# A recurrence that feeds a soft mixture of experts on one core: the last gate moved, one more buffer, the drain put in another order

## The chip, the cores and the metric

The kernel runs on one core of a Trainium2 chip. The core has five engines that run side by side and meet at semaphores: TensorE (PE; its weight loads are listed as PEld), VectorE (DVE), ScalarE (ACT), GpSimd (POOL) and SyncE (SP). SP issues the plain transfers, POOL those that convert float32 to bfloat16 on the way. The metric is the device time of one execution in microseconds (us), as the median of several; lower is better. All other times are us counted from the start of the span of one profiled execution.

## The reference

```python
def _attn_ref(x, f_logit, lower_bound):
    B, S, D = x.shape                                # 4, 5056, 256
    sig = 1.0 / (1.0 + np.exp(-f_logit))
    f = lower_bound + (1.0 - lower_bound) * sig
    i = 1.0 - f
    for t in range(S):
        h = f[:, t] * h + i[:, t] * x[:, t]
        y[:, t] = h
    return y

def _moe_ref(x, phi, w1, w2):                        # x: (20224, 256), E = 8, F = 1024
    logits = x @ phi                                 # 32 slots, 4 for each expert
    d = softmax(logits, axis=0)                      # over all tokens
    slot_input = (d.T @ x).reshape(E, S_per_e, D)
    for e in range(E):
        h = np.maximum(slot_input[e] @ w1[e], 0.0)
        slot_out[e] = h @ w2[e]
    c = softmax(logits, axis=1)                      # over the slots
    return c @ slot_out.reshape(n_slots, D)
```

The softmaxes are written out in the reference; they are shortened here. The output of the recurrence, for all four batches, is the input of the mixture. Because the first softmax runs over all tokens, no output token can be written before the last token has gone through the recurrence and all experts have been computed.

## The kernel before

**Tiling.** The 5056 steps of a batch are cut into 10 groups of 512 (128 partitions times R = 4 steps), the ninth (`odd`, group 8) holding 448. A unit is one group of one batch; unit n is group n // 4 of batch n % 4, 40 units in all. Units are loaded in pairs.

**The steps of a unit**, each a small function: `load` (SP: f_t and x_t, three buffers each), `gate` (ACT: sigmoid of f_t for a pair into s_t), `enter` (POOL: u_t = s_t * x_t), `s_to_channels` and `u_to_channels` (PE: transposes into sp, one buffer of two units, and up, two buffers), `decay` (ACT: a = 1 - (1 - lower_bound) * s, for a pair, one instruction for each half of the channels), `scan` (DVE: the recurrence itself, two instructions, into a buffer of `hpool`), `to_tokens` (PE: transposes of h back, into hp, which has one buffer) and `keep_tokens` (a copy of hp into ht, on DVE for even batches and on ACT for odd ones).

**The steps of a group**: `logits` (PE: phi against h), `exps` (ACT: exponentials for two groups in one instruction, with a table load before them and another when the sigmoid comes back), `weights_to_tokens` (PE transposes, DVE copy into et) and `slots` (PE: accumulates slot_ps).

**The order is written out by hand.** The body of the loop over n names what is issued at step n; each engine executes its own instructions strictly in the order of that text, so a waiting instruction holds up all behind it on its engine. `W_AT` says at which step POOL issues how many of the 16 expert weights (8 of w1, called w0 to w7 below, and 8 of w2, called w8 to w15), each 1 MB of float32 that becomes 0.5 MB of bfloat16. At step 34 the gate of units 38 and 39 and the exponentials of groups 6 and 7 stand ahead of `decay` of 36 and 37, which follows at step 35. `spin` issues matmuls whose results nobody reads.

**The drain** begins with the last scan: logits, exponentials and weights of the last group in two parts (three batches, then the fourth), `left_over` (the 64 odd steps of group 8, four small ACT copies), the last slots, `row_sums` (PE: the denominators of the second softmax), the slot inputs (slot_sb, sin), the w1 products and relu, transposes into `hid`, and the w2 products. Experts 0 to 5 are computed on 32 rows, four at a time, into so4_ps, and are repeated to 128 rows by a matmul with rep; the last W = 2 experts go straight to 128 rows through `wide`, a zeroed array into which their columns are copied. slot_out is the result, on 128 partitions.

**The output**: for each unit, four matmuls of slot_out with the kept exponentials, a scaling on DVE or ACT, and a store by SP.

The lines named below: L183 gate, L194 enter, L209 transposes to channels, L232 decay, L242 scan, L253 and L262 to_tokens and keep_tokens, L286 exps, L121 and L123 weight loads, L128 spin, L554 and L568 w2 products, L572 slot_out, L595 to L632 output.

Of the kernel before, what the change touches and what calls it, by code (L numbers as in the profile page):

```python
# [18 lines left out]
def kernel(  # L19
# [93 lines left out]
    slot_sb = store.tile([P, D], F32, name="slot_sb")  # L113
# [17 lines left out]
    W_AT = {12: 1, 18: 1, 24: 1, 29: 1, 32: 1, 34: 3, 35: 1, 36: 7}  # L131
# [6 lines left out]
    with tc.tile_pool(name="ld", bufs=3) as ld, \  # L138
         tc.tile_pool(name="sp2", bufs=3) as sp2, \
         tc.tile_pool(name="sup", bufs=4) as sup, \  # L140
         tc.tile_pool(name="apool", bufs=2) as apool, \
         tc.tile_pool(name="hpool", bufs=7) as hpool, \
# [6 lines left out]
        slot_ps = pslot.tile([P, D], F32, name="slot_ps")  # L149
# [97 lines left out]
        def to_tokens(n):  # L247
            g, b = divmod(n, B)
            n_p = rows(g)
            hp = ptp.tile([P, R, P], F32, name="hp", tag="tp")  # L250
            hw = hs[n].bitcast(F32).rearrange("c (p r) o -> c p (r o)", r=R)
            for r in range(R):
                nc.tensor.transpose(hp[:n_p, r], hw[:, :n_p, r], ident_f)  # L253
            if b == 0:
                hts[g] = htok.tile([P, B, R, D], BF16, name="ht", tag="ht")
            hps[n] = hp
# [12 lines left out]
        def logits(g, bs=range(B)):  # L269
            T = rows(g) * R  # L270
            gs = batch_of(g)
            if g == gs[0] and bs[0] == 0:
                lgs[0] = plg.tile([P, 2 * G], F32, name="lg", tag="lg")
            lg = lgs[0][:, ds((g - gs[0]) * G, T)]
            for o in range(DC):
                for b in bs:
                    nc.tensor.matmul(lg[ds(b * NS, NS), :], phi[:, o],  # L277
                                     hs[g * B + b][:, :T, o],
                                     start=o == 0, stop=o == DC - 1,
                                     skip_group_check=True)  # L280
# [36 lines left out]
        def left_over():  # L317
            for b in range(B):
                k = ds(b * NS, NS)
                nc.scalar.copy(left[k, :, b % 2], etall[k, ds(odd * G + P * R3, L)])  # L320
# [29 lines left out]
        def late_exps(bs):  # L350
            k = ds(bs[0] * NS, len(bs) * NS)
            nc.scalar.activation(etall[k, ds(last * G, G)], lgs[0][k, :G], ACT.Exp,
                                 accum_out=csum[k, ds(last, 1)])

        def late_weights(bs, copy):
            k, w = ds(bs[0] * NS, len(bs) * NS), len(bs) * NS
            ew = etall[k, ds(last * G, G)].rearrange("s (p r) -> s p r", r=R)
            if bs[0] == 0:
                ets[last] = etok.tile([P, R, B, NS], BF16, name="et", tag="et")
            for r in range(R):  # L360
                nc.tensor.transpose(late_ps[:, r, k], ew[:, :, r], ident[k, k])
            copy(ets[last][:, :, ds(bs[0], len(bs))].rearrange("p r b s -> p r (b s)"),
                 late_ps[:, :, k])

# [26 lines left out]
        for n in range(n_unit):  # L391
# [13 lines left out]
            else:  # L405
                if n % 2 == 0:
                    unit(load, n + AHEAD)
                    unit(gate, n + 4)
                else:
                    unit(decay, n + 1)  # L410
                if n == 34:
                    exps(7)
                elif n != 33:
                    group(exps, n - 2)
# [5 lines left out]

                unit(to_tokens, n - 1)
# [3 lines left out]
                unit(u_to_channels, n + 1)  # L425
                group(logits, n - 1)
            if n == n_unit - 1:
                tail = psp.tile([P, 2, G], F32, name="tail", tag="sp")
                rs_ps = tail[:, 0, ds(0, n_grp * R * B)].rearrange(
                    "p (g r b) -> p g r b", r=R, b=B)  # L430
                late_ps = tail[:, 1].bitcast(BF16)[:, ds(0, R * P)].rearrange(
                    "p (r s) -> p r s", r=R)
                logits(last, [0, 1, 2])
                late_exps([0, 1, 2])
                for g in range(4):
                    row_sums(g)
                late_weights([0, 1, 2], nc.scalar.copy)
                spin(lgs[0][:, ds(G, G)], 2)

            if n in (n_unit - 3, n_unit - 2):  # L440
                spin(lgs[0][:, ds(G, G)], 3)
# [4 lines left out]
            if n == 35:  # L446
                weights_to_tokens(7)
            elif n != 34:
                group(weights_to_tokens, n - 3)
            if n == 36:  # L450
                slots(6)
            elif n == 37:
                slots(7)
            elif n != 35 and n != n_unit - 1:
                batch(slots, n - 4, 0)
                batch(slots, n - 4, 1)
        logits(last, [3])
        late_exps([3])
        left_over()
        to_tokens(n_unit - 1)  # L460
        nc.vector.tensor_copy(hts[last][:, B - 1].rearrange("p r d -> p (r d)").bitcast(F32),
                              hps.pop(n_unit - 1).rearrange("p r c -> p (r c)"))
        late_slots([0, 1])
        late_weights([3], nc.vector.tensor_copy)
        slots(last - 1)
        late_slots([2])
        late_slots([3])
        for g in range(4, n_grp):
            row_sums(g)
        nc.vector.tensor_copy(slot_sb, slot_ps)  # L470

    slot_out = store.tile([P, D], BF16, name="slot_out")
    with tc.tile_pool(name="ew", bufs=1) as ew, \
# [3 lines left out]
        hid = ew.tile([P, FC, E, NS], BF16, name="hid")  # L477
        nc.gpsimd.memset(hid.rearrange("p f e s -> p (f e s)"), 0.0)
        W = 2
        wide = ew.tile([P, FC, W, B, NS], BF16, name="wide")  # L480
        nc.gpsimd.memset(wide.rearrange("p f w b s -> p (f w b s)"), 0.0)
        rep2 = rep.rearrange("p b s -> p (b s)")

        sin_ps = pm.tile([P, DC, NS], F32, name="sin_ps", tag="pm")
        slot_v = slot_sb.rearrange("p (c o) -> p o c", o=DC)
        for o in range(DC):
            nc.tensor.matmul(sin_ps[:, o], slot_v[:, o], rep2[:, :NS],
                             start=True, stop=True, skip_group_check=True)
        spin(tail[:, 1], 3)
        sin = ew.tile([P, DC, NS], BF16, name="sin")  # L490
        for o in range(DC):
            nc.vector.tensor_scalar_mul(sin[:, o], sin_ps[:, o], omlb[:, ds(o, 1)])

        cs1 = ew.tile([P, 1], F32, name="cs1")
        nc.vector.tensor_reduce(cs1, csum, AX.X, ALU.add)

# [21 lines left out]
        nc.tensor.matmul(cs_ps, rep2, cs1, start=True, stop=True)  # L518
        spin(tail[:, 1], 2)
        for q in range(E // Q):  # L520
            ht_ps = psu.tile([P, FC, P], BF16, name="ht_ps", tag="up")
            hi_v = his[q].rearrange("p (c f) -> p f c", f=FC)
            for fc in range(FC):
                nc.tensor.transpose(ht_ps[:, fc], hi_v[:, fc], ident)
            spin(tail[:, 1], 2)

            src = ht_ps.rearrange("p f (j s) -> p f j s", s=NS)[:, :, :, ds(0, SPE)]
            src = bass.AP(tensor=src.tensor, offset=src.offset + q * Q * SPE,
                          ap=[list(src.ap[0]), [P, FC], [NS + SPE, Q], [1, SPE]])
            dst = hid[:, :, ds(q * Q, Q), ds(0, SPE)]  # L530
            dst = bass.AP(tensor=dst.tensor, offset=dst.offset + q * Q * SPE,
                          ap=[list(dst.ap[0]), [E * NS, FC], [NS + SPE, Q], [1, SPE]])
            if q == 0:
                nc.scalar.copy(dst, src)
            else:
                nc.vector.tensor_copy(dst, src)
            for w in range(W):
                e = E - W + w
                if e // Q == q:
                    src = ht_ps[:, :, ds((e % Q) * NS + e * SPE, SPE)]  # L540
                    nc.scalar.copy(wide[:, :, w, :, ds(e * SPE, SPE)],
                                   src.unsqueeze(2).broadcast_to([P, FC, B, SPE]))
        nc.vector.reciprocal(rrow[:, :odd], rs_ps[:, :odd])
        nc.vector.reciprocal(rrow[:, odd, ds(0, R3)], rs_ps[:, odd, ds(0, R3)])
        nc.vector.reciprocal(rrow[:, odd, R3, ds(0, B // 2)], rs_ps[:, odd, R3, ds(0, B // 2)])
        nc.vector.reciprocal(rrow[:, last], rs_ps[:, last])
        rcs = ew.tile([P, 1], F32, name="rcs")
        nc.vector.reciprocal(rcs, cs_ps)


        so4_ps = pm.tile([P, D], F32, name="so4_ps", tag="pm")
        for e in range(E - W):
            for fc in range(FC):
# [3 lines left out]
                                 stop=(e == E - W - 1 and fc >= FC - 4),  # L557
                                 skip_group_check=True)
        spin(tail[:, 1], 2)
# [3 lines left out]
        nc.tensor.matmul(so_ps, rep2, so4, start=True, stop=False, skip_group_check=True)  # L563
        for w in range(W):
            if w == W - 1:
                spin(tail[:, 1], 6)
            for fc in range(FC):
                nc.tensor.matmul(so_ps, wide[:, fc, w].rearrange("p b s -> p (b s)"),  # L568
                                 w2_sb[E - W + w][:, fc],
                                 start=False, stop=w == W - 1 and fc == FC - 1,  # L570
                                 skip_group_check=True)
# [91 lines left out]
```

## Time and profile before

| | us, where no unit stands |
|---|---|
| median of 11 runs (207.26 to 209.84) | 207.95 |
| the profiled execution | 209.07 |
| its span | 207.0 |
| PE busy | 139.1 (67%) |
| DVE busy | 146.5 (71%) |
| ACT busy | 133.8 (65%) |
| POOL busy | 96.5 (47%) |
| read from HBM, as the page counts it | 58.23 MB |
| written to HBM, as the page counts it | 20.71 MB |

The busy times are averages over three stages: units 0 to 39 (to about 134 us), the drain (to about 150 us), and the output (to the end). No engine is busy for more than 71% of the whole. The page's second part cuts the span into 40 slices of 5.175 us; a digit is a share in tenths, and 9 stands for 90% or more. "PEclk" is the TensorE clock that was granted, "DMA" the mean share of the core's 16 DMA engines. A row of the timeline has the start, the time that the merged instructions take from first start to last end, engine, line and operation, and in brackets how long the engine had been idle before it and what is taken to have released it. A row of the view by stretches of time has the stretch, its length, the busy times of PE, PEld, DVE, ACT and POOL (with the number of instructions in brackets), the granted clock, the DMA share and GB/s.

### The profile page before, as it was taken

The page shows a single profiled execution, that of the slowest core. Times are in us where ns is not written, and L with a number is a line of the kernel's source. Part 1 is how long each engine was busy: PE and PEld are TensorE (multiplying, and loading weights), DVE is VectorE, ACT ScalarE, POOL GpSimd, SP SyncE. Part 2 cuts the span into 40 slices and gives each one's busy share as a digit, 9 for nine tenths or more (in the row PEclk, how much of TensorE's full clock was granted, in tenths as well). Part 3 has the DMA queues.
Part 4 walks back from the last instruction along what each step waited for, and adds up shares of the span by engine and source line. Part 5 has one row for each costly group of instructions (what it writes and reads, how often), then busy time and mean ns, then how long its engine had stood idle before and what let it go on. Part 6 is the DMA issues. An engine that isn't in the chain of part 4 may idle for free.

```text
span 207.0 us, 3138 instructions
## 1 busy us (share of the span) xinstructions
PE 139.1 (67%) x1107; PEld 95.5 (46%) x1107; DVE 146.5 (71%) x166; ACT 133.8 (65%) x183; POOL 96.5 (47%) x65
## 2 busy tenths in 40 slices
PE   0657567676769587675867379999946778775700
PEld 0336336654657465564755376666532333321300
DVE  1677549889997999999799839944283756554540
ACT  3575799699996999899886665333055454564230
POOL 1555769964997299946985999100000000000000
PEclk9999979799996999998899969999995555555555
DMA  5999999999999999999999999999049999999995
GB/s 188 416 412 408 409 411 407 410 409 407 406 313 420 401 327 417 406 312 403 403 322 352 251 210 212 215 214 194 5 176 370 407 405 407 408 406 407 398 395 230
DMA packets 21039, 70.75 MB, mean 342 GB/s; under 512 B 2592, under 2 KB 3360, under 8 KB 21024
## 3 DMA queue, kind: packets, MB, share of 16 engines
q1 hardware_dynamic: 18432, 62.14, 75.9%
q0 software_dynamic: 2304, 8.39, 20.3%
q8 instruction: 8, 0.13, 0.2%
q10 hardware_dynamic: 288, 0.03, 0.1%
q14 instruction: 7, 0.06, 0.1%
HBM read 58.23 MB, written 20.71 MB: 381 GB/s over the span
## 4 chain that ended last, share of the span: by engine, by line
PE 31%; DVE 25%; DMA 15%; ACT 13%; issue 9%; SPq 2%; POOL 1%; DVEq 0%; ACTq 0%
DVE h L242 15%; DMA out_dram<-ob 13%; PE hp L253 8%; PE sp L209 6%; DVE ob L601 6%; ACT s_t L183 5%; DVE ht L262 4%; PE up L209 4%; ACT a L232 3%; SPq L632 2%; DMA f_t<-in_f_logit_dram 2%; PE tail L128 2%; ACT ob L606 1%; PE op L595 1%; ACT L286 1%
## 5 line engine op out<-in xcount | busy, mean ns | idle before, releaser
L194 POOL TENSOR_TENSOR u_t<-s_t,x_t 128x1024 bf16<-128x1024 bf16 (+1 forms) x39 | 82.1, 2129 | 27.4 <-ACT s_t L183 18.5
L242 DVE TENSOR_TENSOR_SCAN h<-a,h,up 128x512 bf16<-128x512 f32 (+1 forms) x72 | 86.2, 1250 | 7.0 <-PE up L209 4.0
L232 ACT ACTIVATE a<-sp,nomlb 128x1024 f32<-128x1024 bf16 (+2 forms) x46 | 43.4, 996 | 12.5 <-PE sp L209 9.2
L253 PE MATMUL hp<-ident_f,h 128*128 128x128 f32 (+1 forms) x160 | 31.6, 325 | 29.2 <-DVE ht L262 16.5
L606 ACT ACTIVATE ob<-op,rrow 128x256 f32<-128x256 f32 x63 | 24.6, 477 | 30.0 <-DVE ob L601 18.3
L601 DVE TENSOR_TENSOR ob<-op,rrow 128x1024 f32<-128x1024 f32 (+2 forms) x25 | 28.2, 1148 | 20.3 <-DMA out_dram<-ob 16.7
L183 ACT ACTIVATE s_t<-f_t 128x2048 bf16<-128x2048 f32 (+2 forms) x23 | 38.4, 1672 | 5.7 <-DMA f_t<-in_f_logit_dram 3.0
L595 PE MATMUL op<-slot_out,etall 32*128 32x256 bf16 x156 | 32.8, 378 | 13.3 <-ACT ob L606 10.9
L253 PEld LDWEIGHTS hp<-ident_f,h 128*128 128x128 f32 (+1 forms) x160 | 23.2, 208 | 39.6 <-DVE ht L262 21.2
L209 PE MATMUL sp<-ident_f,s_t 128*128 128x128 f32 x144 | 24.3, 319 | 10.0 <-ACT s_t L183 8.9
L595 PEld LDWEIGHTS <-etall 32*128 32x128 bf16 x156 | 13.9, 122 | 31.7 <-issue 27.1
L209 PE MATMUL up<-ident_f,u_t 128*128 128x128 f32 x144 | 25.3, 304 | 4.1 <-POOL u_t L194 4.0
L209 PEld LDWEIGHTS sp<-ident_f,s_t 128*128 128x128 f32 x144 | 20.4, 168 | 11.1 <-issue 5.8
L209 PEld LDWEIGHTS up<-ident_f,u_t 128*128 128x128 f32 x144 | 19.3, 159 | 6.2 <-POOL u_t L194 5.5
L262 DVE COPY ht<-hp 128x512 f32<-128x512 f32 (+1 forms) x20 | 13.4, 671 | 7.4 <-PE hp L253 7.4
L262 ACT COPY ht<-hp 128x512 f32<-128x512 f32 (+1 forms) x19 | 11.1, 586 | 6.2 <-PE hp L253 6.2
L242 DVE TENSOR_TENSOR_SCAN h<-a,up 128x512 bf16<-128x512 f32 x8 | 9.2, 1206 | 1.2 <-PE up L209 1.2
L277 PE MATMUL lg<-h,phi 128*32 128x512 bf16 (+1 forms) x80 | 7.5, 425 | 0.0
L183 ACT ACT_TABLE_LOAD x4 | 5.1, 1283 | 1.7 <-PEq L647 1.7
L327 PE MATMUL slot_ps<-ht,et 128*32 128x256 bf16 (+1 forms) x144 | 5.9, 288 | 0.0
L286 ACT ACT_TABLE_LOAD x4 | 5.1, 1283 | 0.1
L121 POOL DMA_DIRECT2D w_sb<-in_moe_w_dram x8 | 4.8, 600 | 0.0
(85 smaller groups left out, 86.9 us busy)
## 6 DMA issues: line engine op xcount, KB each, us to landing
f_t<-in_f_logit_dram SPq DMA_DIRECT2D x36, 512.0 KB, 10.1
x_t<-in_x_dram SPq DMA_DIRECT2D x36, 512.0 KB, 9.7
out_dram<-ob SPq DMA_DIRECT2D x34, 512.0 KB, 5.6
w_sb<-in_moe_w_dram POOLq DMA_DIRECT2D x16, 512.0 KB, 9.1
f_t<-in_f_logit_dram SPq DMA_DIRECT2D x4, 384.0 KB, 8.8
x_t<-in_x_dram SPq DMA_DIRECT2D x4, 384.0 KB, 7.9
out_dram<-ob SPq DMA_DIRECT2D x4, 384.0 KB, 4.7
out_dram<-ob SPq DMA_DIRECT2D x4, 256.0 KB, 4.1
```

What stands on the lines that cost most here:

```text
L183: nc.scalar.activation(s_t, f_t, ACT.Sigmoid, scale=-1.0)
L194: nc.gpsimd.tensor_tensor(uts[n][:, :r], s_t[:, :r], x_t[:, :r], ALU.mult)
L209: nc.tensor.transpose(ps[:, :, r], t[:, r], ident_f)
L232: nc.scalar.activation(decays[n // 2, o][:, ds(n % 2, k), :T], sp[:, ds(n % 2, k), :T, o], ACT.Identity, scale=nomlb[:, ds(o, 1)], bias=1.0)
L242: nc.vector.tensor_tensor_scan(h[:, :T, o], decays[n // 2, o][:, n % 2, :T], up[:, :T, o], hs[n - B][:, ds(used(n // B - 1) - 1, 1), o] if ...
L253: nc.tensor.transpose(hp[:n_p, r], hw[:, :n_p, r], ident_f)
L262: copy(hts[g][:n_p, b].rearrange("p r d -> p (r d)").bitcast(F32), hps.pop(n)[:n_p].rearrange("p r c -> p (r c)"))
L277: nc.tensor.matmul(lg[ds(b * NS, NS), :], phi[:, o], hs[g * B + b][:, :T, o], start=o == 0, stop=o == DC - 1, skip_group_check=True)
L286: nc.scalar.activation(etall[:, ds(gs[0] * G, T)], lgs[0][:, :T], ACT.Exp, accum_out=csum[:, ds(g, 1)])
L595: nc.tensor.matmul(op[:, r], ew[ds(b * NS, NS), :, r], slot_out[ds(b * NS, NS), :], start=True, stop=True, skip_group_check=True)
L601: nc.vector.tensor_tensor(ob[:, ds(r, k)], op[:, ds(r, k)], scale[:, ds(r, k)].broadcast_to([P, k, D]), ALU.mult)
L606: nc.scalar.activation(ob[:, r], op[:, r], ACT.Copy, scale=scale[:, r])
```

## The change

The change has these parts.

- The gate of units 38 and 39 and the exponentials of groups 6 and 7 are issued at step 35, behind `decay` of units 36 and 37. The steps that follow from them move too: weights_to_tokens of group 7 and slots of group 6 to step 37; logits and exponentials of group 8, left_over, slots of group 7 and the weights of group 8 to step 38, where u_to_channels stands ahead of to_tokens.
- `hpool` has eight buffers for seven. To make room, the last group's ht, `hid`, `wide` and slot_sb take over buffers that are no longer used.
- One weight load moves from step 36 to step 33.
- left_over goes from ACT to POOL; the copy of unit 39's tokens from DVE to ACT; half of sin and of the copies into `wide` change engines; the largest reciprocal and the column sums come earlier.
- The spins of steps 37 to 39 and of the expert stage go, but for two; `idle`, four matmuls into an unread half of slot_ps's bank, is added at steps 35 and 36.
- The w2 products: experts 0 to 3 on 32 rows, experts 4 to 7 straight to 128 rows; the repeat by rep comes behind the first of these.

The diff, cut to its core:

```diff
-    W_AT = {12: 1, 18: 1, 24: 1, 29: 1, 32: 1, 34: 3, 35: 1, 36: 7}
+    W_AT = {12: 1, 18: 1, 24: 1, 29: 1, 32: 1, 33: 1, 34: 3, 35: 1, 36: 6}
...
-         tc.tile_pool(name="hpool", bufs=7) as hpool, \
+         tc.tile_pool(name="hpool", bufs=8) as hpool, \
...
+        def idle(k):
+            for _ in range(k):
+                nc.tensor.matmul(slot_bank[:, 1], w1_sb[0][:, 0, :P], w1_sb[0][:, 0, :D],
+                                 start=False, stop=False, skip_group_check=True)
...
-                nc.scalar.copy(left[k, :, b % 2], etall[k, ds(odd * G + P * R3, L)])
+                nc.gpsimd.tensor_copy(left[k, :, b % 2], etall[k, ds(odd * G + P * R3, L)])
...
+        def odd_weights():
+            n_p = rows(odd)
+            ets[odd] = etok.tile([P, R, B, NS], BF16, name="et", tag="et")
+            ew = etall[:, ds(odd * G, n_p * R)].rearrange("s (p r) -> s p r", r=R)
+            for r in range(R):
+                nc.tensor.transpose(odd_ps[:n_p, r], ew[:, :, r], ident)
+            nc.scalar.copy(ets[odd][:n_p].rearrange("p r b s -> p r (b s)"), odd_ps[:n_p])
...
+                end = n >= n_unit - 6
                 if n % 2 == 0:
                     unit(load, n + AHEAD)
-                    unit(gate, n + 4)
+                    if not end:
+                        unit(gate, n + 4)
                 else:
                     unit(decay, n + 1)
-                if n == 34:
-                    exps(7)
-                elif n != 33:
+                    if n == n_unit - 5:
+                        gate(n + 3)
+                        exps(odd - 1)
+                if not end and n != n_unit - 7:
                     group(exps, n - 2)
...
+                if n in (n_unit - 5, n_unit - 4):
+                    idle(4)
+                if n == n_unit - 2:
...
+                    logits(odd)
+                    exps(odd)
+                    left_over()
+                    slots(odd - 1)
+                    spin(tail[:, 1], 1)
+                    odd_weights()
...
-            if n in (n_unit - 3, n_unit - 2):
-                spin(lgs[0][:, ds(G, G)], 3)
...
+            if n == n_unit - 3:
+                weights_to_tokens(odd - 1)
+                slots(odd - 2)
...
-        left_over()
         to_tokens(n_unit - 1)
-        nc.vector.tensor_copy(hts[last][:, B - 1].rearrange("p r d -> p (r d)").bitcast(F32),
-                              hps.pop(n_unit - 1).rearrange("p r c -> p (r c)"))
-        late_slots([0, 1])
+        keep_tokens(n_unit - 1)
         late_weights([3], nc.vector.tensor_copy)
-        slots(last - 1)
-        late_slots([2])
+        slots(odd)
+        late_slots([0, 1, 2])
         late_slots([3])
...
-        for e in range(E - W):
+        for e in range(Q):
...
-        spin(tail[:, 1], 2)
         so4 = ew.tile([P, D], F32, name="so4")
         nc.vector.tensor_copy(so4, so4_ps)
         so_ps = pm.tile([P, D], F32, name="so_ps", tag="pm")
-        nc.tensor.matmul(so_ps, rep2, so4, start=True, stop=False, skip_group_check=True)
-        for w in range(W):
-            if w == W - 1:
-                spin(tail[:, 1], 6)
+        for j in range(Q):
             for fc in range(FC):
-                nc.tensor.matmul(so_ps, wide[:, fc, w].rearrange("p b s -> p (b s)"),
-                                 w2_sb[E - W + w][:, fc],
-                                 start=False, stop=w == W - 1 and fc == FC - 1,
+                nc.tensor.matmul(so_ps, wide[:, fc, j].rearrange("p b s -> p (b s)"),
+                                 w2_sb[Q + j][:, fc],
+                                 start=j == 0 and fc == 0, stop=j == Q - 1 and fc == FC - 1,
+                                 skip_group_check=True)
+            if j == 0:
+                nc.tensor.matmul(so_ps, rep2, so4, start=False, stop=False,
                                  skip_group_check=True)
```

## The prediction

> **What bounds the kernel now.** Times are us from the span's start; "unit n" is the n-th of 40 (group, batch) pieces. I read the page's slices first. They show a kernel that is a transfer at both ends with a hole between:
>
> ```profile
> PEclk9999979799996999998899969999995555555555
> DMA  5999999999999999999999999999049999999995
> ```
>
> Every slice from the second on has its DMA engines full, until two empty ones (144.9 to 155.3). Before the hole the inputs and then the expert weights stream in, behind it 20.7 MB stream out. No edit makes the streams smaller, so only the hole can shrink: from the last weight's landing to the first stores. Stretches of time, with the last column in GB/s and the one before it the share of the DMA engines, give its edges:
>
> ```profile
> 116.00:118.00 2.00, 0.17 (x2) 0.00 (x0) 1.99 (x3) 1.98 (x2) 1.53 (x4) 1.00 0.83 221
> ...
> 134.00:144.00 10.00, 9.99 (x136) 6.11 (x137) 4.38 (x11) 3.79 (x11) 0.00 (x0) 1.00 1.07 215
> 144.00:145.00 1.00, 1.00 (x40) 0.98 (x44) 0.96 (x3) 0.42 (x2) 0.00 (x0) 1.00 0.42 78
> 145.00:146.00 1.00, 1.00 (x19) 0.30 (x11) 0.70 (x5) 0.00 (x0) 0.00 (x0) 1.00 0.11 25
> 146.00:152.00 6.00, 4.37 (x40) 3.01 (x41) 1.42 (x3) 0.21 (x1) 0.00 (x0) 1.00 0.00 0
> ```
>
> The reader is to see one small earlier loss (0.83 at 116 to 118) and the stream running dry at 144 to 146 while PE (second number) is busy. The last weight, w15, is issued at 125.95 and its view says:
>
> ```profile
> L123 POOL DMA_DIRECT2D w_sb<-in_moe_w_dram x1: 535/535/535, 126.0 to 126.0; - x1
> ...
> DMA to landing us min/median/max: 20.1/20.1/20.1
> ```
>
> It lands at 126.0 + 20.1 = 146.05, w14 and w13 (18.6 and 16.7) at 143.6 and 141.2. The timeline then shows w15 waiting for PE, not PE for w15:
>
> ```profile
> 147.36 1.46 PE L128 MATMUL tail<-w_sb 128*128 128x512 bf16 x6
> 148.44 0.97 PEld L568 LDWEIGHTS <-wide 128*128 128x128 bf16 x8
> 148.66 1.04 PE L568 MATMUL so_ps<-w_sb,wide 128*128 128x256 bf16 x8
> ...
> 149.73 0.48 DVE L572 TENSOR_SCALAR slot_out<-so_ps,rcs 128x256 bf16<-128x256 f32 x1 [3.83 <-PE so_ps L568]
> ```
>
> So the compute chain is 2.6 late (148.66 against 146.05). The chain of waits leads from there back through the drain to units 36 and 37:
>
> ```profile
> 117.44 1.28 ACT L286 ACT_TABLE_LOAD   x1
> ...
> 118.73 1.02 ACT L286 ACTIVATE etall<-lg 128x1024 bf16<-128x1024 f32 x1
> ...
> 119.75 0.58 ACT L262 COPY ht<-hp 112x512 f32<-112x512 f32 x1
> ...
> 120.38 0.98 PE L253 MATMUL hp<-ident_f,h 128*112 128x128 f32 x4 [4.20 <-ACT ht L262]
> ...
> 121.40 0.69 DVE L262 COPY ht<-hp 112x512 f32<-112x512 f32 x1 [3.00 <-PE hp L253]
> ```
>
> Ahead of the table load ACT stood 2.66 before the gate of 38/39 (L183, 115.51 to 117.42). The row names POOL, but the f_t load it needs was issued at 101.3 and took 14.1: it landed about then. The copy of unit 33, ready since 114.9, queues behind gate, table and exponentials; PE (single hp buffer) and DVE wait for it. DVE is idle 118.40 to 121.40 and 122.09 to 123.10: 4.0.
>
> **The gate and exponentials behind the decays.** New ACT order: copy 33 at 114.9 to 115.5; decays 36/37 when PE's sp is done (115.7, then 2.13 as at 120.21) to 117.83; gate 1.91 to 119.74; table and exponentials 2.33 (117.42 to 119.75 before) to 122.07; copy 35; decays 38/39 from 122.5 to 124.7. DVE: the scans of 34/35 end at 118.40 as before, copy 34 follows at once (its transposes can run at 116.3), scans of 36/37 (2.45 each) 119.1 to 124.0, copy 36, the et copy, scans of 38/39 from 125.5 to 130.4. Before, the last scan ended at 134.37: **4.0 less**. What is late next: u of 38 (POOL, 2.13 each) starts at 119.8 and not 117.56, u of 39 ends at 124.8; scan 39 wants it at 127.9, so this is covered by 2. The exponentials queue ahead of copy 35, so hp of 36 starts at 122.7; its DVE copy cannot start before 124.0 anyway. Cost 0. The two groups of 4 idle matmuls (128x256, about 0.11 each by L568's 1.04 for 8) lie before waits of PE: 0.
>
> **Eighth h buffer.** Logits of group 8 move from unit 36 to 38, so h of 32 is read until about 128; with seven buffers scan 39 would wait for it. With eight: 0.
>
> **One weight issued earlier (w5 behind u of 36).** Its issue (0.59) delays u of 37 from 115.43 to 116.05, wanted at 120.9. It fills the loss at 115 to 118, about 0.5, so the whole weight queue should end 0.5 sooner: w15 at 145.55; lower end of the gain 0 (146.05). Against it, the Trainium skill ("DMA: Bandwidth & Descriptors", Queues, rings and completion order) says that each engine goes round its queue rows packet by packet: w5 would take half the rate from the last f_t. By the rule f_t lands up to 1.1 later (half of 113.4 to 115.5), at 116.6; by the row it need not, as w4 (issued 108.0, landed 117.2) already holds that queue. The gate now wants f_t at 117.83: 0 by either.
>
> **Drain.** From 130.4, with durations of the old rows: copy 38 on DVE 131.85; PE's hp 38, logits of three batches and ACT's exponentials to 132.35; row sums, late weights and their copy to 133.2; logits and exponentials of the last batch to 133.85; copy 39, now on ACT, to 134.45; slots 8 (0.55) and sixteen late slots (0.6) to 135.25; twelve row sums beside them, the slot copy and sin to 136.5; rest of the row sums and one spin to 136.95; w1 products 1.9 to 138.85; relu and transposes to 140.1; four experts on 32 rows (32 of 48 matmuls of 1.42) to 141.05; w12's 8 matmuls 0.9, the repeat 0.45, then 0.9 each for w13, w14 and w15. Without any load PE would end at 145.1. Removed are 25 spins (about 0.22 each, those of the drain 3.7 in sum); added are two wide experts, 16 full matmuls for 16 narrow ones, about +1.3. left_over on POOL (four 32x64 copies, no row; between 0.1 and 1 each, from 64 of u's 1024 columns at 2.13 up to the old ACT row's scale, 1.08 for all four; I take 0.3, nearest to that row) and the two memsets (hid 0.9 and wide 3.7, by 1.83 for 2048) end near 134.2; they are wanted at 139.4: 0, and if left_over were 1 each, still 0. The csum and reciprocal moves lie beside PE's w1 products: 0.
>
> **Sum.** PE reaches w14 in time, ends it at 144.2, and waits for w15: 145.55 + 0.1 + 1.04 gives 146.6 where the old row ends at 149.7: **3.1 less**, or 2.6 if the queue isn't filled. From slot_out on everything is as before (57.3 to the end, DMA full). Of the 4.6 that compute saves (149.7 to 145.1), 1.5 to 2 go into the new wait. I take 2.9. The profiled execution took 209.07 (span 207.0), so it would take 206.2; the shown median is 207.95, 1.1 below it, so **205.0**.
>
> **The clock.** A rule speaks against taking spins away: the skill ("TensorE: Matmul & The Clock Gate", Why this matters for your kernels) warns of PE idle gaps beyond some 3 us. The longest new gap is 1.4 (144.2 to 145.6), so by the rule the clock stays at 1.00. The trace is stricter: it fell to 0.50 at about 154.9, with no gap over 1.7 before it, PE being busy only some 38% of the 3.4 before. Ahead of w15 I count 2.1 of 3.4 (62%), nearer to warm. Cold would cost the last 8 matmuls 8 x 0.243 (the cold op row, 1.94 for 8) for 1.04, and the first half tile 0.4: 1.3 in all.
>
> **Rivals.**
> - Cold before w15, as priced: 206.3. For it: if the drain is 1 us quicker than summed, PE waits for w14 too and the busy share falls to 35%. Chance 0.13.
> - The compute chain slips more than 1.5 past 145.1 (single hp buffer in the order ACT copy 37, PE hp 38, DVE copy 38, or the tail's bank shared by row sums and sin), so that w15 waits for PE again; with a slip of 3 PE ends at 148.1 and 1.6 is left: 206.3. Against it: scan 39 has to be over 1.5 late. Chance 0.09.
> - The wait is smaller than I think: the weights' stream ends sooner, compute ends it at 145.1: 4.6 less, 203.4. Against it: the DMA engines have no free slot but the one at 116. Chance 0.06.
> - Slower: without spins the clock falls at the start of the drain and stays at 0.50. Drain matmuls without spins are some 9 us warm; at half speed all of them add up to 9 to the chain, which then ends at 154: 4.4 later, 212.3. It decides once over 4.6 of them are added, half the drain cold. For it: 0.50 at 120.8 to 124, after 4.2 of idleness. Against it: no such gap is left. Chance 0.05.
> - The change doesn't do what it says, the gate's wait just moving to u of 39 or to POOL: about 207.9. Chance 0.04.
>
> **Numbers.** The likeliest has 0.63; its own range is 204.4 to 205.7 (0.5 for the fill, some 0.4 for how the stores start). The range for 8 in 10 adds part of both 206.3 cases: 204.2 to 206.5. A measurement of this kernel can tell about 0.5%, 1.04, from no change: faster 0.88, same 0.06, slower 0.06.
>
> **What would show it.** Right: DVE without the 3.0 idle near 118; the last scan near 130.4; w15's matmuls released by its DMA near 145.6, clock 1.00; slot_out near 146.7. Wrong: w15 landed well before its matmuls start; a clock of 0.5 between 125 and 146; a scan of 38 or 39 waiting for u; the weights' last packets still at 146 or later.

## The result and the profile after

| | before | after |
|---|---|---|
| median on the same chips, us (runs) | 208.74 (47) | 206.74 (12) |
| lowest and highest | 207.26, 211.46 | 204.88, 210.55 |
| ratio after / before, 95% interval | | 0.9892 (0.986 to 0.9923) |
| profiled execution; its span | 209.07; 207.0 | 205.18; 203.4 |
| last scan ends | 134.37 | 130.02 |
| last weight lands | 146.05 | 145.1 |
| slot_out starts | 149.73 | 146.42 |

The changed kernel is faster by 1.1% (0.8 to 1.4), which on 207.95 is 205.7; forecast were 205.0 and a range of 204.2 to 206.5. The profiled execution gained more: 3.9. Ratios leave out executions over 1.5% above the fastest of their kernel, so a ratio is not always the quotient of the medians.

First the slices of the page, to be held against the two rows shown of before:

```profile
PEclk9999988998896999999699999999985555555555
DMA  6999999999999999999999999999369999999995
```

There are still two slices that are not full, but now 3 and 6 stand for 0 and 4: the hole is shorter. The stretches of time (length; busy PE, PEld, DVE, ACT, POOL; clock; DMA share; GB/s) give its edges:

```profile
116.00:118.00 2.00, 1.83 (x16) 1.46 (x14) 1.99 (x3) 1.92 (x2) 1.96 (x4) 1.00 1.08 281
...
143.00:144.00 1.00, 1.00 (x8) 0.76 (x7) 0.01 (x1) 0.00 (x0) 0.00 (x0) 1.00 0.68 139
144.00:145.00 1.00, 1.00 (x11) 0.90 (x10) 0.00 (x0) 0.00 (x0) 0.00 (x0) 1.00 0.17 33
145.00:146.00 1.00, 1.00 (x11) 0.89 (x10) 0.00 (x0) 0.00 (x0) 0.00 (x0) 1.00 0.00 0
```

The loss at 116 to 118 is gone (1.08 for 0.83). The stream runs dry one stretch sooner, and beside it PE (second number) is busy without a break. The last weight, w15, is the second of the two issues here; it starts at 127.6 and has the longest flight, 17.5, so it lands at 145.1:

```profile
L122 POOL DMA_DIRECT2D w_sb<-in_moe_w_dram x2: 567/571/575, 127.1 to 127.6; - x2
...
DMA to landing us min/median/max: 15.6/16.5/17.5
```

The timeline of after shows the rest (start, time, operation, in brackets the idle time before it and its releaser):

```profile
118.58 0.66 DVE L272 COPY ht<-hp 112x512 f32<-112x512 f32 x1
...
125.22 4.79 DVE L247 TENSOR_TENSOR_SCAN h<-a,h,up 128x512 bf16<-128x512 f32 x4
...
137.19 0.25 DVE L521 TENSOR_SCALAR sin<-tail,omlb 128x32 bf16<-128x32 f32 x1 [1.40 <-PE tail L127]
...
137.50 2.07 PE L539 MATMUL hi_ps<-w_sb,sin 128*32 128x512 bf16 x32 [0.42 <-DVE sin L521]
...
143.60 2.78 PE L591 MATMUL so_ps<-w_sb,wide 128*128 128x256 bf16 x24
...
146.42 0.49 DVE L598 TENSOR_SCALAR slot_out<-so_ps,rcs 128x256 bf16<-128x256 f32 x1 [3.41 <-PE so_ps L591]
```

The copy of unit 34 (118.58) follows its scans with no bracket, where before DVE waited 3.0 for that place. Of the 4.35 that the last scan gained, the first w1 product (L539) kept 1.97: it comes 7.48 behind the last scan, where before it came 5.10 behind: there the transposes of unit 38 (131.59) ran 2.8 ahead of the last scan's end, here (130.09) just behind it. From there to slot_out it is 8.92 for 10.26, which gives back 1.34, and slot_out is 3.31 sooner. The 24 products of w13 to w15 are one unbroken row to 146.38. The last eight, a third of it, start near 145.45, 0.35 after w15 has landed: nobody waits for the weight, and the weight has hardly waited for PE. The output is as before, 57.0 from slot_out to the end for 57.3.

### The profile page after: what moved, and what is told of

Same layout as the page of the kernel before. It is cut to its first block, busy times and chain, and to the rows that moved or that the text cites. A ratio compares the mean times of both kernels' runs of the same rounds, so it can differ in the third digit from the quotient of the medians.

```text
span 203.4 us, 3111 instructions
## 1 busy us (share of the span) xinstructions
PE 135.0 (66%) x1092; PEld 93.3 (46%) x1092; DVE 145.6 (72%) x165; ACT 134.2 (66%) x182; POOL 98.5 (48%) x69
## 4 chain that ended last, share of the span: by engine, by line
DVE 34%; PE 24%; DMA 16%; ACT 12%; issue 9%; POOL 1%; SPq 1%; DVEq 0%; ACTq 0%
DVE h L247 22%; DMA out_dram<-ob 14%; DVE ob L627 6%; ACT s_t L188 5%; PE sp L214 5%; PE hp L258 5%; DVE ht L272 4%; ACT a L237 3%; PE up L214 3%; DMA f_t<-in_f_logit_dram 2%; PE so_ps L591 2%; PE slot_ps L336 2%; ACT ob L632 1%; PE op L621 1%; ACT ht L272 1%
## 5 line engine op out<-in xcount | busy, mean ns | idle before, releaser
L258 PE MATMUL hp<-ident_f,h 128*128 128x128 f32 (+1 forms) x160 | 31.2, 322 | 28.9 <-DVE ht L272 17.5
L214 PE MATMUL sp<-ident_f,s_t 128*128 128x128 f32 x144 | 22.9, 306 | 10.0 <-ACT s_t L188 9.0
L214 PEld LDWEIGHTS sp<-ident_f,s_t 128*128 128x128 f32 x144 | 19.2, 161 | 11.4 <-issue 5.8
L272 ACT COPY ht<-hp 128x512 f32<-128x512 f32 (+1 forms) x20 | 11.7, 585 | 4.3 <-PE hp L258 4.1
L336 PE MATMUL slot_ps<-ht,et 128*32 128x256 bf16 (+1 forms) x144 | 6.4, 304 | 0.8 <-DVE et L310 0.8
L295 ACT ACTIVATE etall<-lg 128x1024 bf16<-128x1024 f32 (+1 forms) x5 | 4.6, 927 | 2.7 <-PE lg L286 2.7
```

The costliest lines, as they stand in the source:

```text
L214: nc.tensor.transpose(ps[:, :, r], t[:, r], ident_f)
L272: copy(hts[g][:n_p, b].rearrange("p r d -> p (r d)").bitcast(F32), hps.pop(n)[:n_p].rearrange("p r c -> p (r c)"))
L295: nc.scalar.activation(etall[:, ds(gs[0] * G, T)], lgs[0][:, :T], ACT.Exp, accum_out=csum[:, ds(g, 1)])
L336: nc.tensor.matmul(slot_ps[ds(b * NS, NS), :], et[:n_p, r, b], ht[:n_p, b, r], start=(g == 0 and r == 0), stop=(g == n_grp - 1 and r == R ...
```

## The experiments

They ran on three chips, each beside the kernel before (medians there 209.15, 209.34 and 209.18), so ratios are compared, and traces where a mechanism is meant. In the texts of what was expected, theory A and its rivals are the two or three outcomes that each run was to tell apart.

**The gate and exponentials back ahead of the decays, all else changed.**

```diff
-                    if not end:
+                    if not end or n == n_unit - 6:
                         unit(gate, n + 4)
+                    if n == n_unit - 6:
+                        exps(odd - 1)
...
-                    if n == n_unit - 5:
-                        gate(n + 3)
-                        exps(odd - 1)
```

> The changed kernel with one part undone: the gate of units 38 and 39 and the exponentials of groups 6 and 7 stand ahead of the decays of 36 and 37 again; everything else stays changed. Theory A (the move is what pays): ACT gets to the copy of unit 33 some 4.3 us later, DVE stands idle for about 3 near 118 and the scans of 36 start near 122.3 for 119.2; the last scan ends near 133.4 for 130.0, and PE's last w2 product near 149.8 for 146.4, so the time is that of the kernel before, a ratio of 0.997 to 1.004. Rival B (the drain's edits pay, the scans' end being hidden by the weights' landing): the ratio stays within 0.003 of the changed kernel's 0.989.

Ratio 0.9959 (0.9898 to 1.0021), as theory A had it. It rests on four of the twelve executions; the median of all twelve is 210.79. Its timeline, first the recurrence, then the drain:

```profile
115.18 1.91 ACT L188 ACTIVATE s_t<-f_t 128x2048 bf16<-128x2048 f32 x1 [2.25 <-DMA f_t<-in_f_logit_dram]
...
120.87 0.69 DVE L272 COPY ht<-hp 112x512 f32<-112x512 f32 x1 [2.39 <-PE hp L258]
...
128.62 4.78 DVE L247 TENSOR_TENSOR_SCAN h<-a,h,up 128x512 bf16<-128x512 f32 x4
...
140.88 3.56 PE L538 MATMUL hi_ps<-w_sb,sin 128*32 128x512 bf16 x32 [0.41 <-DVE sin L520]
...
151.29 0.49 DVE L597 TENSOR_SCALAR slot_out<-so_ps,rcs 128x256 bf16<-128x256 f32 x1 [3.41 <-PE so_ps L590]
```

The old stall is back in its old place: ACT waits 2.25 for f_t, now put down to the DMA by name, DVE waits 2.39 for the copy behind it, and the last scan ends at 133.40, 3.38 later than in after. The scans of 34 and 35 start at 114.10 here and 114.28 there, so nothing ahead of the edit makes the difference. slot_out is even 4.9 later, as here the w1 products also took 3.56 for 2.07: the granted clock was 0.50. With the old recurrence the other edits gain nothing that can be told. The interval overlaps that of the change, so it is the trace that shows what the gate's move does, and not the ratio.

**The expert stage of before** (six experts on 32 rows, two wide, its spins), with the new recurrence:

```diff
-        spin(tail[:, 1], 1)
+        W = 2
+        spin(tail[:, 1], 3)
...
-        for e in range(Q):
+        for e in range(E - W):
...
+            if w == W - 1:
+                spin(tail[:, 1], 6)
```

> The changed kernel with the expert stage of before: six experts on 32 rows, two straight to 128, and its 17 spins. Theory A (the spins and the product's form lie on PE's path): 16 more spins at 0.22 are +3.5, 16 narrow products for 16 full ones -1.3, so PE's last product moves from 146.4 to about 148.6 and the ratio from 0.989 to about 1.000. Rival B (the spins only fill waits of PE, and the last ones wait for the last weight's landing anyway): PE's end moves by less than 0.7 and the ratio stays below 0.993. Rival C (the spins keep the clock up and the changed kernel pays for their loss): faster than 0.986.

Ratio 0.9942 (0.9898 to 0.9987), between what theory A and rival B had. The last scan ended at 129.16 and w15 landed at 145.3, yet slot_out starts at 147.35. The timeline has the reason:

```profile
144.98 1.46 PE L127 MATMUL tail<-w_sb 128*128 128x512 bf16 x6
...
146.27 1.04 PE L599 MATMUL so_ps<-w_sb,wide 128*128 128x256 bf16 x8
```

Six spins lie over the landing. From last scan to slot_out this drain takes 18.19, that of after 16.40: the new stage is 1.8 shorter, of which slot_out shows 0.9, as the last scan here ended 0.86 sooner. The intervals of the two ratios just overlap.

**The kernel before without its 25 spins**, everything else as before:

> The kernel before without its 25 spins, nothing else changed. Theory A: some spins fill waits (those before sin, hid and so4), the 6 before the last weight's products and 2 between the transposes do not; PE's end falls from 149.7 to about 147.5, bounded below by the last weight's landing near 146.05 plus 1.04; ratio 0.988 to 0.993, so either half of the change reaches the same bound alone. Rival B (the spins hold the clock): the granted clock falls to 0.50 somewhere between 130 and 150 and the ratio is 1.00 or more.

Ratio 0.9928 (0.9888 to 0.9968). The timeline:

```profile
114.81 1.91 ACT L183 ACTIVATE s_t<-f_t 128x2048 bf16<-128x2048 f32 x1
...
120.41 0.69 DVE L262 COPY ht<-hp 112x512 f32<-112x512 f32 x1
...
129.86 2.44 DVE L242 TENSOR_TENSOR_SCAN h<-a,h,up 128x512 bf16<-128x512 f32 x2
...
148.42 1.03 PE L559 MATMUL so_ps<-w_sb,wide 128*128 128x256 bf16 x8 [2.17 <-DMA w_sb<-in_moe_w_dram]
```

PE is early, stands 2.17 and is released by w15; in this execution the stream was late and w15 landed at 148.3. The spins of before thus cost some 0.7% (0.3 to 1.1), though the clock in this profile was 0.50 from 129.8 to 136.2, where that of before was 1.00. By the ratios alone, taking out the spins can't be told from the whole change.

The first three rows show what the profile of before could not. The recurrence runs 2.1 behind (the scans of 34 and 35 start at 116.09, for 114.02 before), and the old stall is not there, though the gate stands ahead of the decays: ACT doesn't wait for f_t, the copy of unit 34 follows its scans at once, and the last scan ends at 132.30, 2.1 sooner than in the profile of before. (The first of the spins that are gone stood at 127.7 there, behind all this.) So the wait of 3.0 that the gate's move takes away is found in some executions of the old order and not in all.

**No load of w15** (its products read the weight of expert 6), in the changed kernel:

```diff
+        if i == 2 * E - 1:
+            return
...
-                                 w2_sb[Q + j][:, fc],
+                                 w2_sb[min(Q + j, E - 2)][:, fc],
```

> The changed kernel without the load of the last weight (the w2 of the last expert; the w2 of the one before is used in its place, so that part of the result is left out). Theory A (in the changed kernel PE just reaches the last weight when it lands, 145.1 against 145.4): PE's end and the time stay as they are, within 0.3 us of the changed kernel. Rival B (the wait for the last weight bounds the end, as predicted): the weights end 2.4 sooner, PE's end falls by about 1 us or more, and the ratio goes below 0.985.

Ratio 0.9882 (0.9814 to 0.995), median 207.37 of 6: no gain that can be told, though with so wide an interval one of 1 us isn't excluded. That the compute chain is as late as the weight is read from the trace of after. The profiled execution here took 210.35, with clock 0.50 from 133.8 to 144.0.

**The changed kernel once more, and with filler in PE's waits:**

```diff
+                    idle(8)
...
+                idle(1)
...
+        idle(3)
...
-        spin(tail[:, 1], 1)
+        spin(tail[:, 1], 2)
```

> The changed kernel once more, unaltered, for a second profile and for a baseline beside the next three. Theory A (the clock in the drain decides between executions): over several executions the changed kernel falls to 0.50 somewhere between 129 and 146 in some and not in others, so this profile either repeats the first (1.00 throughout, drain of 16.4 from the last scan to slot_out) or shows a cold stretch and a drain of 17.5 to 19.5; median ratio again 0.987 to 0.992. Rival B (the drain is always warm and the spread comes from the recurrence and the transfers alone): drain 16.2 to 16.6 whatever the total.

> The changed kernel with 13 more matmuls nobody reads, only where PE waits in its drain: 8 of 128x256 before the transposes of unit 38 (a wait of 1.16), 1 before the late weights, 3 behind the transposes of unit 39 (0.4), 1 of 128x512 before the w1 products (0.4). Theory A (without spins the clock falls in some executions of the drain, and this is what keeps the median above the profiled gain): clock 1.00 from 125 to 146, drain below 16.8, and the median ratio falls to 0.983 to 0.988, with less spread. Rival B (the clock isn't the cause, the matmuls only lengthen PE's path): the ratio stays at 0.989 or rises to 0.992.

The same kernel again: 0.9943 (0.9903 to 0.9983), above the 0.987 to 0.992 that was expected. Its profile took 206.43, 1.25 more than the first one's, and this is where it went, by stretches and in the timeline:

```profile
138.00:139.00 1.00, 1.00 (x16) 0.46 (x12) 0.59 (x1) 0.60 (x1) 0.00 (x0) 0.51 1.08 217
139.00:140.00 1.00, 1.00 (x16) 0.34 (x8) 0.69 (x1) 0.02 (x1) 0.00 (x0) 0.50 1.00 201
140.00:141.00 1.00, 1.00 (x12) 0.34 (x5) 0.22 (x1) 0.58 (x1) 0.00 (x0) 0.50 1.08 217
```

```profile
137.38 3.36 PE L539 MATMUL hi_ps<-w_sb,sin 128*32 128x512 bf16 x32 [0.41 <-DVE sin L521]
...
147.63 0.48 DVE L598 TENSOR_SCALAR slot_out<-so_ps,rcs 128x256 bf16<-128x256 f32 x1 [3.41 <-PE so_ps L591]
```

The last scan (129.91) and w15 (145.5) are those of the first profile. The w1 products take 1.29 more, and slot_out is 1.21 later: the difference is the clock. With filler the profile stayed at 1.00 through the drain, and w15's products waited for the weight:

```profile
145.31 1.03 PE L594 MATMUL so_ps<-w_sb,wide 128*128 128x256 bf16 x8 [0.38 <-DMA w_sb<-in_moe_w_dram]
```

There slot_out started at 146.39. But its ratio, 0.9926 (0.9877 to 0.9976), and its median, 207.02 for 206.96, are no better that can be told. So the clock explains the difference of two profiles; how much of the spread of all executions it makes isn't settled.

**w5 issued late, as before:**

```diff
-    W_AT = {12: 1, 18: 1, 24: 1, 29: 1, 32: 1, 33: 1, 34: 3, 35: 1, 36: 6}
+    W_AT = {12: 1, 18: 1, 24: 1, 29: 1, 32: 1, 34: 3, 35: 1, 36: 7}
```

> The changed kernel with the weight loads issued as before: w5 at step 34 and seven at step 36. Theory A (the early issue fills a gap of the DMA engines at 115 to 118): the DMA share falls to 0.7 to 0.9 there, w15 lands 0.4 to 1.0 later (145.5 to 146.1), PE waits for it, and the ratio rises by 0.001 to 0.004 over the changed kernel beside it; more in executions whose recurrence lags by 2, since POOL issues w5 to w7 only behind u of 37. Rival B (transfers are full anyway): same landing within 0.2, same ratio.

Ratio 0.9921 (0.9868 to 0.9975), within the interval of the change. In the profiled execution, which took 208.54, the recurrence lagged 1.8, and the weights queued on POOL behind u of 37 with it. In the view by stretches the DMA share falls where the queue ran empty:

```profile
117.00:118.00 1.00, 1.00 (x12) 0.98 (x10) 1.00 (x2) 0.66 (x2) 1.00 (x2) 1.00 0.24 74
118.00:119.00 1.00, 0.83 (x8) 0.63 (x6) 0.99 (x2) 1.00 (x2) 1.00 (x3) 1.00 0.54 45
119.00:120.00 1.00, 0.94 (x9) 0.63 (x7) 1.00 (x2) 1.00 (x2) 0.15 (x1) 1.00 0.57 90
```

That is 1.65 lost (0.76 + 0.46 + 0.43), and w15 landed at 148.3. The profile without w15, above, lagged as much but has w5 early: there the share fell in one stretch only, to 0.64 at 117 to 118. What the early weight does is thus seen, a transfer that doesn't hang on the recurrence; what it is worth on the median is not.

**A version with slack.** In after ACT copies the weights of group 8 ahead of the tokens of unit 37, and hp has one buffer, so unit 38's transposes wait, though its scans end at 127.6:

```profile
130.09 0.75 PE L258 MATMUL hp<-ident_f,h 128*128 128x128 f32 x4 [1.16 <-ACT ht L272]
```

The change is to swap the two:

```diff
                     spin(tail[:, 1], 1)
-                    odd_weights()
...
+            if n == n_unit - 2:
+                odd_weights()
```

It was run on two chips, on the second also with w15's load cut into two halves, and without w15.

> The changed kernel with the copy of unit 37's tokens ahead of the copy of group 8's weights on ACT. Theory A (between the last scan and the last batch's exponentials PE and ACT wait for each other through the single hp buffer): the transposes of unit 38 start near 128.9 for 130.1, PE reaches the last weight's products about 1.1 sooner, and waits there for w15's landing near 145.1, so a warm execution gains only 0.2 to 0.4 and a cold one up to 1.1: ratio 0.984 to 0.988. Rival B (the end of the last scan, 130.0, sets the drain): no gain, same drain of 16.4 and the changed kernel's ratio.

> The version with the copy of unit 37 first, unaltered, as a baseline beside the next two and with more executions. Theory A (its drain reaches the last weight 1.4 early, so that a cold stretch of the clock is absorbed by the wait): PE waits for w14 or w15, slot_out near 1.1 after w15's landing, median ratio 0.982 to 0.987 and little spread. Rival B (the first six executions were lucky): ratio of the changed kernel, 0.989 or above.

> The same with the last weight's load cut into two halves of four matmuls each. Theory A (the last landing bounds the end): when the second half lands only 4 matmuls are left instead of 8, slot_out comes about 0.6 after the landing instead of 1.1, a gain of 0.4 to 0.5, ratio 0.002 below the kernel beside it. Rival B (a second issue and its own completion cost as much, or the tail of both halves lands together): no gain within 0.001, or a landing later by 0.3 or more.

> The version with the copy of unit 37 first, without the load of the last weight (the w2 of the expert before is used in its place, so that part of the result is left out). Theory A (the landing of w15 is what ends the drain): PE needs only w14, near 142.8, and ends its last product at about 144.9 in place of 146.3; the time falls by 1.2 to 1.6, ratio 0.975 to 0.981. Rival B (PE's own chain ends the drain): no change within 0.5 us.

| | median (6 runs each; lowest, highest) | ratio (95%) | slot_out |
|---|---|---|---|
| swapped | 205.83 (205.41, 206.24) | 0.989 (0.9834 to 0.9945) | 146.34 |
| swapped, second chip | 205.22 (205.13, 205.34) | 0.9876 (0.9835 to 0.9917) | 146.28 |
| w15 in halves | 205.28 (204.71, 206.29) | 0.9888 (0.9833 to 0.9943) | 146.13 |
| without w15 | 203.80 (203.57, 204.20) | 0.9811 (0.9768 to 0.9853) | 144.96 |

The timeline of the second row is the picture that the prediction had drawn of the change itself:

```profile
142.75 1.03 PE L592 MATMUL so_ps<-w_sb,wide 128*128 128x256 bf16 x8 [0.64 <-DMA w_sb<-in_moe_w_dram]
...
145.21 1.03 PE L592 MATMUL so_ps<-w_sb,wide 128*128 128x256 bf16 x8 [1.42 <-DMA w_sb<-in_moe_w_dram]
...
146.28 0.48 DVE L599 TENSOR_SCALAR slot_out<-so_ps,rcs 128x256 bf16<-128x256 f32 x1 [5.79 <-PE so_ps L592]
```

PE stands 0.64 for w14 and 1.42 for w15, 2.06 in sum. Of that the swap made some 1.3 (from last scan to the first w1 product 6.17, in after 7.48); the rest is a recurrence that ended at 128.81 in this execution. slot_out is where it was, 0.14 sooner. Without w15, slot_out comes right behind its products:

```profile
142.04 2.88 PE L594 MATMUL so_ps<-w_sb,wide 128*128 128x256 bf16 x24
144.96 0.48 DVE L601 TENSOR_SCALAR slot_out<-so_ps,rcs 128x256 bf16<-128x256 f32 x1 [3.51 <-PE so_ps L594]
```

1.32 earlier, and 1.42 less in the median, though the recurrence ended 1.0 later in this execution (129.79): here the landing of w15 is what ends last. Halving its load gives nothing that can be told, as the second half lands at 145.4, no sooner than the whole (145.2).

**Seven h buffers**, all else changed:

```diff
-         tc.tile_pool(name="hpool", bufs=8) as hpool, \
+         tc.tile_pool(name="hpool", bufs=7) as hpool, \
```

> The changed kernel with seven h buffers. The buffer of unit 39 is then that of unit 32, which logits of group 8 still read until about 127.6, while the scan of 39 wants it at 127.7. Theory A (the eighth buffer covers next to nothing where it stands now): last scan later by 0 to 0.3, ratio that of the changed kernel within 0.002. Rival B (the buffer is needed): DVE waits 0.5 or more ahead of the scan of 39, and the ratio rises by 0.003 or more.

Ratio 0.99 (0.9849 to 0.9951). Its last scans show no wait:

```profile
125.67 4.82 DVE L247 TENSOR_TENSOR_SCAN h<-a,h,up 128x512 bf16<-128x512 f32 x4
```

The eighth buffer is worth nothing measurable here. The profile was again a cold one, w1 products 3.32, slot_out 148.22.

## Why the prediction was right, and which term was off

- **The gate behind the decays: right.** Last scan forecast for 130.4, measured 130.02, and 133.40 with this step alone undone. u of 39 ended at 125.0 (forecast 124.8) and held nothing up. What the prediction took for granted is that the old order always stalls: the kernel before without spins, in an execution that lagged, had no such wait.
- **Eighth h buffer, 0: half right.** The cost was 0, but the reason given, that with seven buffers scan 39 would wait, was wrong: the scans run without a break with seven.
- **w5 early: right in kind, low in size.** The share at 116 to 118 is full, w15 landed at 145.1 for a forecast of 145.55. Landings of 145.2 to 145.5 in eight other profiles with w5 early show it to be steady. The f_t that was weighed against it came no later: with the gate in front ACT had it at 115.18, for 115.51 before.
- **Drain: the term that was mis-sized.** "Without any load PE would end at 145.1" measured 146.38, 1.3 more. Up to the slots the sum held within 0.1 (135.29 for 135.25). Then sin, summed to run beside the row sums, waited 1.40 for the last matmul into `tail`, the tile that it shares with them, the spin. (With two spins there, in the run with filler, it waited 1.62, and with three, in the old expert stage, 1.83.) The w1 products started at 137.50 for 136.95 and took 2.07 for 1.9. Relu and transposes took until 141.08 for 140.1, and 0.3 came after. So the forecast wait of 1.5 to 2 for w15 did not exist. The two misses met: weight 0.45 sooner, chain 1.3 later, and slot_out at 146.42 for 146.7. That the place came out so near is luck; the wait that the prediction drew as its cause was not there. The 3.1 of the sum measured 3.3. left_over took 1.13 in all (four of 0.28) and the memsets 0.95 and 3.51, over by 133.9, hidden as said.
- **Clock: the step that failed.** It was priced at 1.3 with a chance of 0.13, and looked for ahead of w15, where PE would wait. The measured 1.29 agrees by luck, as it is of other matmuls: the clock falls at the w1 products. It does so in five of the six profiles with the change's drain (the change again, gate back, seven buffers, w5 late, no w15: w1 products 3.05 to 3.56), all but the first. In the six with another drain (old expert stage, filler, the four swapped ones) it stays at 1.00 and they take 1.91 to 2.08.
- **From the profile to the median: off by 0.7** (205.7 for 205.0). The profiled execution of before was put 1.1 above the median of the runs shown; over 47 runs it is 0.33 above. The gain of 2.9 is 1.4%, a ratio of 0.986, the edge of the interval; 1.1% was measured. The first profile, with a warm drain, gained 3.9 and lies 1.56 below its kernel's median, about as far as a cold stretch costs. That fits the clock as the cause of the missing part; it isn't shown, since the filler did not win it back. A second candidate was not tried: executions of the old order that lag and so have no stall, where the gate's move has less to gain.
- **Rivals.** "The compute chain slips more than 1.5" came near with 1.3 and cost nothing, as the weight landed just ahead of it. "The wait is smaller" was so, but by slower compute. "Slower because the clock stays at 0.50 through the whole drain" is refuted for the median, as the stretch ends after 3 to 4 in four of the five cold profiles; but the profile without w15 was cold for 10 and took 210.35, and two of the twelve executions of the change took about as long (209.86 and 210.55), so it may well happen in some. "Doesn't do what it says" is refuted by the experiment on the gate.

The swapped order beats both kernels in the median (205.22 and 205.83, against 206.74 and 206.96 for the change). The ratios' intervals overlap. What its slack can do is absorb a cold stretch of 1.3. That fits twelve executions between 205.13 and 206.24, against 204.88 to 210.55 for twelve of the change, but no cold profile of this version was caught to show it. All four were at 1.00 through the drain, so that this order may as well be one that keeps the clock up; no run separates the two.

Left open: why the recurrence lags by 2 in some executions, how often the clock falls, and why the filler improved no median. In two of the three profiles with that lag (no spins, w5 late) it stands at 32 already, long before anything that the edits touch, with scans at 32.25 and 32.23 for 30.20 before: between 18 and 27 the rows of four transposes took 1.06 to 1.13, where before has 0.60 to 0.75. But the profile with seven buffers starts as slowly and has caught up by 114. In the third (no w15) the clock was 0.50 from 110 to 113.

## What to carry to other kernels

When compute and a transfer end within a microsecond of each other, look at both before the next edit: take the transfer away, shorten the compute, then do both, and the numbers say which ends last. Move a long instruction that waits for a load behind the short ones that others wait for, and follow each queue it passes: here one swap of two copies on ACT shortened the drain by another 1.3, of which the landing let only the spread show. Filler matmuls are judged by where they lie: six of them in the kernel before stood in front of a weight that had landed, and held its products up by 1.3; but a profile without any fell to a clock of 0.50. And one profile shows one execution: a stall seen in it may be missing from others, so a gain forecast from it is the gain of that execution.

## What was not expected of the hardware

The Trainium skill ("TensorE: Matmul & The Clock Gate", Why this matters for your kernels) asks for no PE idle gaps beyond some 3 us, and the prediction added a row of its own, 38% busy. Neither foresees this. In the 3.4 before 138.0, PE was busy for 2.93 with 65 matmuls in the warm profile and for 2.93 with 65 in the cold one; the longest gap from 126 on was 1.16 in both; one stayed at 1.00 and the other fell to 0.50. Many of these matmuls are tiny: 23 row sums of 128x4 each, and 128x32 or 32 rows elsewhere; whether that matters no run here shows. Busy time alone doesn't tell the clock. That the same program falls to either side fits the page's statement (Part 1, What's actually happening) that the window in which activity is counted runs free of the kernel's start; no run here shows the window.

The landing of the last weight does not move with its issue. In after it is issued at 127.6 and flies 17.5, in the swapped version at 126.4 and 18.8, in the kernel without the gate's move at 125.9 and 19.4; it lands at 145.1, 145.2 and 145.3. In each the DMA share is near 1.05 until close to the landing, so that an earlier issue only flew longer. Where the share had a gap, at 117 to 120 with w5 late and at 117 to 119 in the kernel before without spins, the landing was at 148.3.
